# A window-attention and squared-ReLU kernel: a second batch through seven half-size products, the sinks' values in 64-row matmuls, and a written-out order

## The chip, the cores and the metric
One core of one Trainium2 chip runs the whole kernel in one launch. The metric is device time in microseconds (us), the median of three executions. The profiler recorded one execution more. TensorE (PE, with its weight loads PEld) multiplies; VectorE (DVE), ScalarE (ACT) and GpSimd (POOL) work on tiles; SyncE (SP) only issues transfers, and POOL and ACT can issue some as well. SBUF is the on-chip memory, PSUM the 8 accumulator banks of 2 KB a partition that matmuls write to.

## The reference
Four batches, eight heads, 768 positions, 64 channels a head. A query sees the 128 newest keys up to its own and the first four keys ("sinks"). The result, as 3072 rows of 512, goes through two dense layers with a squared ReLU between.
```python
scores = q @ k.T / 8                     # (4, 8, 768, 768)
keep = (key < 4) | ((0 <= query - key) & (query - key < 128))
a = softmax(where(keep, scores, -1e9))
x = (a @ v).transpose(0, 2, 1, 3).reshape(3072, 512)
h = x @ w_in                             # 512 x 2048
out = maximum(h, 0) ** 2 @ w_out         # 2048 x 512, float32
```
Inputs and output are float32 in DRAM.

## The kernel before
**Units.** A batch is 6 query tiles of 128, taken as 3 pairs of tiles; its 8 heads are 4 pairs of heads m = 0 to 3, the two heads of a pair lying in partitions 0-63 and 64-127. Matmuls take bf16.

**Loads.** Batch 0's first four tiles of q and k come by eight SP loads ("qr", L557). Everything else comes by loads that POOL issues and that turn float32 into bf16: tiles of q and k (L578, and L606 for batches 2 and 3), of v (L587, L616), w_in in four parts of 512 KB (L514), w_out in four quarters of 512 KB (L522). POOL's order is: v tiles 0 and 1, w_in part 0, v 2 and 3, w_in parts 1 to 3, k and q tiles 4 and 5, v 4 and 5, w_out 0 to 3, then batch 1 (k, q, v), 2 and 3.

**Attention.** q and k are transposed: batches 0 and 1 on TensorE against `ident` (L708; regrouped first for the SP-loaded ones, copied from PSUM afterwards, L397 to L403), batches 2 and 3 by SP's transposing DMAs (L662). Scores of a pair of heads (L815) are matmuls over 64 rows, one head in each half of the array; ScalarE takes exp (L836); VectorE (L845) or POOL (L426) masks it. Batch 0's first pair of tiles gets its mask as a bias instead, by matmuls with `ident` (L808). The scores of the four sink keys of all heads stand in 32 rows for each pair of heads (L774), their exp in `es` (L782); `vs` holds the sinks' v, zero outside the rows that belong to a head (L756).

**Values** (L884), one PSUM bank a pair of heads: for each head and each of two query tiles up to three matmuls of 65 columns (64 channels and the row sum), the last of them over the sinks, with all 128 rows of `es` and `vs`:
```python
if t >= 2:
    mms.append((i, h2, es[:, 128 * (t - 2):128 * (t - 2) + 128], vs[:, h, :]))
```
VectorE divides (L900, L901). The result is transposed into `xT` by TensorE (L933, a "bridge", batches 0 and 1) or by SP's DMAs (L915, batches 2 and 3).

**First dense layer.** Batches 0 to 2: plain matmuls (L965), 256 columns for batch 0, 512 for the first two pairs of the others and 256 for the third; relu L976 (ACT) or L978 (DVE), square L985 (ACT) or L987 (DVE). Batch 3, named by `FAST = (3,)`: Strassen's seven half-size products. Five sums of quarters of w_in are made once (L1009), four sums of x for each part (L1043, the first a "spread" copy for the single pair); then `quad` makes groups of seven products (L1085): product 1 is copied away (L1126), products 2 and 5 are subtracted from the copy, 4 and 3 are accumulated on 2 and 5, relu (L1141) and square (L1107 on ACT, L1109 on DVE) give two of four blocks, and products 6 and 7 with an add-and-clamp (L1153) and a second square give the other two. A batch has six groups: two of 128 columns for one pair of tiles, four of 256 for two pairs.

**Second dense layer.** The first two pairs of tiles of batch 0 plainly (L1174, store L1197), all others by seven products in Winograd's form: sums of w_out L1215, sums of the squares L1242, products L1284, PSUM combinations L1309 to L1332, stores L1352 to L1371.

**Order.** Every step is registered in a class `Plan` with its engine, modelled cost, dependences and buffers; `Plan.run` then places the steps one after the other by a list scheduler with modelled times, after a table `SHIFTS` has moved the due times of single steps. That gives each engine's program order. `warm` (L386 to L395) puts unneeded matmuls ("dummies", L393) into modelled gaps of TensorE near the start, 63 in all. PSUM is two pools of two tiles of two banks, `den` (dense layers) and `att` (attention). In SBUF `expm` has 8 buffers, `r` 3, `sg` 4; a pool gives its buffers in turn.

Of the kernel before, what the change touches and what calls it, by code (L numbers as in the profile page):

```python
# [12 lines left out]
FP32 = mybir.dt.float32  # L13
BF16 = mybir.dt.bfloat16
# [3 lines left out]
LATENCY = 0.135  # L18
PE_SLACK = 0.0
DMA_START = {"sp": 1.45, "act": 1.2, "pool": 1.6}  # L20
DMA_LATENCY = 0.9
WARM_UNTIL = 34.0
SHIFTS = {
    None: ((-0.254, -0.2), (-0.571, -0.26), (-3.153, 0.8), (-0.345, -0.74), (-0.83, 3.28), (-0.98, -0.76),
        (1.458, 1.69), (-1.232, 0), (0.55, -0.13), (-1.841, -0.16), (-0.527, -1.31), (-1.271, -0.72), (-0.963, 0.32),
        (0.605, -2.77), (-1.323, 1.3), (-1.6, 0.58), (-2.678, -2.44), (-1.476, -0.28), (-2.561, -0.7),
        (-1.331, -0.42), (-1.151, -0.2), (-1.253, -0.22), (-0.398, -0.87), (0.902, 2.55), (-1.318, -0.7),
        (-1.389, -0.4), (-1.246, -0.74), (-0.947, 8.2), (-1.272, 0.2), (-0.428, -2.57), (-1.738, 0), (-1.257, -0.22),
        (-0.151, -1.78), (0.73, -2.69), (-1.258, -0.08), (-1.109, 1), (-1.269, -0.18), (-0.332, -1.95),
        (-1.198, 0.88), (-1.403, -0.28), (-0.085, 0.43), (-1.257, -0.22), (-1.492, -0.14), (-1.966, -0.82),  # L30
        (-1.228, 2.28), (-0.609, -0.3), (-1.172, -0.72), (-0.948, 1.33), (-1.214, -0.14), (-0.818, 0.07),
        (0.509, 0.34), (-1.258, 0.66), (-1.614, 0.1), (-0.282, -0.76), (-0.521, -1.37),),
    ('prep', 0, 0): ((-0.212, 1.23), (-0.072, -0.24), (-0.19, 0.16), (-0.726, 0.34), (0.102, 1.1), (-0.535, 0.02),
        (-0.602, -0.59), (0.354, 0.3), (-3.718, -4.59), (0.634, 0.85), (-0.293, -1.06), (-1.346, -1.52),
        (-0.272, 0.1), (0.418, -0.32), (-0.151, 0.16), (-0.447, -0.7), (0.314, -0.72), (0.319, 0.77), (-0.551, 0.09),
        (-0.072, 0.2), (-0.13, 0.16), (0.105, 0.24), (1.083, 0.83), (0.872, 0.89), (-0.583, 0.42), (-0.732, -0.4),),
    ('sink', 0, 0): ((4.752, 1.43), (1.667, 2.03),),
    ('att', 0, 0): ((0.347, 0.31), (0.954, 0.9), (-0.499, -1.83), (0.762, -2.15), (0.932, -0.05), (-2.305, -7.94),
        (-0.09, 0.64), (-0.608, -0.19),),
    ('val', 0, 0): ((-0.669, 0.31), (-0.697, -0.27), (2.439, -2.91), (-0.554, 0.35), (-0.437, -0.15), (-0.471, 0.35),  # L40
        (-0.386, 0.35), (-0.377, 0.25),),
    ('turn', 0, 0): ((1.726, 0.79), (1.562, 0.69), (1.948, 1.13), (1.496, 0.73),),
    ('att', 0, 1): ((3.244, 0.46), (11.783, 1.08), (3.403, 0.48), (2.622, -0.1), (0.081, -0.49), (-0.044, -0.15),
        (11.287, 1.58), (1.317, -0.32), (2.357, -0.58), (1.537, 1.18), (-0.135, 0.19), (-0.111, -0.81),),
    ('val', 0, 1): ((-1.139, 2.3), (-0.295, 1.56), (-0.887, 1.68), (-0.625, 1.18), (-3.257, -5.22), (-3.374, -3.06),
        (-3.291, -3.92), (-2.551, -2.62),),
    ('turn', 0, 1): ((0.396, -1.51), (-0.815, -0.63), (-0.017, -0.23), (-0.694, 0.15), (-0.252, 1.39),),
    ('prep', 0, 1): ((0.244, -0.3), (0.839, 0.68), (-0.246, 0.32), (0.932, -0.62), (1.027, -0.56), (0.209, -0.32),),
    ('sink', 0, 1): ((1.975, -1.87), (0.782, -1.52),),
    ('att', 0, 2): ((0.244, -0.66), (-1.989, 0.29), (-0.493, 0.33), (0.159, -0.68), (1.032, 0.54), (0.796, 0.57),  # L50
        (-0.189, 0.02), (1.388, -0.12), (0.48, -0.01), (0.313, -0.14), (1.032, 0.72), (-1.933, -0.09),),
    ('val', 0, 2): ((-0.074, -1.39), (-0.782, 0.91), (-0.843, -3.97), (-0.333, 0.47),),
    ('turn', 0, 2): ((0.672, -0.31), (-0.118, -0.09), (0.809, -0.71), (2.596, 0.84),),
    ('l1', 0, 0): ((1.946, 1.98), (2.477, 2.05), (2.842, 0.55), (1.744, 2.15), (1.004, -3.64), (-0.401, 3.09),
        (1.762, -0.33), (2.032, -0.69), (0.818, -0.26), (0.463, 0.08), (2.529, 0.93), (3.08, -0.59),),
    ('l1', 0, 1): ((-1.505, -0.48), (0.385, 0.7), (-1.5, -0.46), (0.416, -0.68), (-0.498, 0.3), (-0.582, 0.6),
        (-0.46, -0.02), (-0.566, -0.1), (0.513, -0.12), (-0.444, -0.02), (-1.914, 1.12), (-0.022, 0.42),),
    ('l1', 0, 2): ((1.159, -0.13), (1.171, -0.31), (4.523, 0.49), (0.77, -0.87), (1.53, -0.41), (0.926, -0.79),
        (0.522, -0.76), (1.124, -0.01), (1.066, -0.47), (4.319, 0.45), (0.749, -2.99), (0.301, -1.88),),
    ('prep', 1, 0): ((-3.284, 0.24), (-1.096, -0.94), (0.605, -0.58), (0.247, -2.12), (-5.483, 0.49), (0.694, 0.02),  # L60
        (0.597, -0.24), (0.597, -0.24), (-8.208, 1.17), (0.681, -1.4), (-1.5, -0.64), (0.357, -0.54), (-10.29, 0.97),
        (0.494, -0.72), (0.633, -0.24), (-0.776, -0.16), (0.529, -0.04), (-1.768, -0.84),),
    ('sink', 1, 0): ((0.868, 0.19), (0.763, 0.03),),
    ('att', 1, 0): ((-0.287, -0.2), (-4.964, -0.65), (-1.435, -0.81), (-3.607, -0.91), (-2.001, -0.01),
        (-0.447, -0.1), (-0.674, 0.1), (-0.719, -0.6), (-0.604, 0.18), (-0.781, -0.2),),
    ('val', 1, 0): ((-6.954, 1.31), (0.072, -4.26), (-0.107, -0.44), (-0.058, -0.46),),
    ('turn', 1, 0): ((-4.522, 0.82), (-0.734, 2.5), (-1.073, 0.44), (0.276, 0.05),),
    ('att', 1, 1): ((1.003, 0.22), (1.223, 0.6), (0.413, -0.45), (0.232, -0.07), (0.259, -0.21), (0.322, -0.07),
        (1.914, -1.56), (0.055, 0.01), (0.085, -2.03), (0.176, 0.47),),
    ('val', 1, 1): ((0.205, 0.29), (-0.249, -0.53), (-2.761, 0.71), (0.377, -0.27),),  # L70
    ('turn', 1, 1): ((0.754, 1.22), (2.068, -0.78), (0.857, 1.68), (-4.788, 1.81),),
    ('prep', 1, 1): ((2.397, 1.96), (5.859, 1.94), (-0.449, 1.75), (1.83, 1.58), (1.97, 1.7), (0.173, -0.21),),
    ('sink', 1, 1): ((0.987, -0.02), (-0.036, -5.62),),
    ('att', 1, 2): ((1.119, -4.28), (0.959, -0.36), (0.499, 1.02), (0.438, -0.34), (1.738, -0.38), (0.767, 0.25),
        (1.547, -0.3), (1.332, 0.31), (1.014, 0.54), (0.269, -2.08),),
    ('val', 1, 2): ((1.128, -0.41), (3.047, 0.37), (3.469, 0.88), (2.416, -3.47),),
    ('turn', 1, 2): ((-4.356, -7.65), (-0.607, -0.19), (-1.006, 0.46), (-4.587, -4.53),),
    ('wt', 0): ((-0.423, 0.42), (-0.315, 0.14), (-1.716, 1), (-0.361, 0.06),),
    ('l2', 0, 0): ((6.071, 1.48), (1.943, -1.23), (2.592, 0.39), (0.401, -1.21), (5.784, 0.74), (5.992, 1.58),
        (2.993, -2.81), (2.732, 0.86), (0.489, -0.39), (-0.516, -1.21), (2.415, 0.45),),  # L80
    ('l2', 0, 1): ((-0.438, 1.25), (-0.215, 0.46), (-0.282, 0.35), (0.307, -0.75), (-0.329, 0.71), (0.749, -0.74),
        (0.871, 0.46), (0.785, 0.08), (0.702, 1.69), (-0.352, 0.8), (2.254, -2.28),),
    ('sum', 0, 2): ((0.045, -1.68), (0.204, -1.02), (-0.718, -2.55), (0.064, -1.38),),
    ('l2', 0, 2): ((0.177, 0.43), (0.08, 0.05), (0.043, -0.01), (0.087, 0.13), (0.146, -0.05), (0.286, 0.01),
        (-3.566, 0.64),),
    ('ev', 0, 2): ((0.387, -2.73), (0.215, -1.01), (-0.063, -1.45), (-0.129, -4.69), (0.419, -1.95), (0.228, -0.91),
        (-0.334, -3.43), (0.529, -0.75),),
    ('l1', 1, 0): ((-2.25, 1.33), (0.301, 1.9), (2.02, -1.38), (0.412, 0.1), (0.164, 0.26), (0.039, -0.22),
        (0.926, -8.17), (-0.524, 0.12), (0.373, 0.12), (1.304, 1.55), (1.015, 0), (0.579, -0.12), (0.204, -0.09),
        (0.523, 0.4), (-0.028, -0.17), (-1.901, 0.85), (0.353, 0.12), (0.196, 0.02), (-1.978, -2.11), (1.417, -0.02),  # L90
        (0.319, -0.99), (0.194, -4.07), (-3.291, 0.39), (0.291, 2.35),),
    ('l1', 1, 2): ((2.497, -0.43), (3.349, 0.01), (2.786, -0.17), (2.851, -0.17), (2.812, 1.03), (0.807, 1.08),
# [106 lines left out]
        (0.268, 1.28),),  # L199
    ('ev', 3, 2): ((1.463, 6.42), (-1.377, 1.64), (0.142, -5.03), (-0.286, -3.32), (-0.494, 0.4), (-0.624, -0.94),  # L200
        (-0.804, -0.94), (-1.227, -0.94), (-0.047, -3.46),),
}


class Slot:
# [16 lines left out]
class Plan:  # L222

# [1252 lines left out]
```

## Time and profile before

| | us |
|---|---|
| median of three executions | 217.82 (217.82, 218.05, 216.72) |
| profiled execution: span from the first to the last instruction | 216.0 |
| busy: PE / PEld / DVE | 206.5 / 165.4 / 161.5 |
| busy: ACT / POOL | 123.2 / 98.7 |
| landed: the last of the eight q and k loads of SP | 11.3 |
| landed: v 0, v 1, w_in part 0 | 11.8, 12.8, 16.2 |

The profiled execution's own time is its span; the median of the executions is 1.8 above it. How to read the lines shown below: in a wait's line stand the waiting engine, tile and line, what it waited for, and then the us in all, the number of times, and the longest. In the chain of work that ended last a line has a start, a length and what ran. A window's line has its two ends, its length, the busy time of PE, PEld, DVE, ACT and POOL with their instructions, the granted TensorE clock, the share that the transfers kept the DMA engines busy (over 1 when several stand queued), and GB/s. A timeline's line has start, length, engine, kernel line, operation, tile and operands. A group's line has line, engine, operation, operands, count, then busy us and mean ns of one, then the idle time before them and who ended it. A matmul's record is longer than its share of the pipeline: what one costs in a row is the distance of the starts.

### The profile page before, as it was taken

The page shows a single profiled execution, that of the slowest core. Times are in us where ns is not written, and L with a number is a line of the kernel's source. Part 1 is how long each engine was busy: PE and PEld are TensorE (multiplying, and loading weights), DVE is VectorE, ACT ScalarE, POOL GpSimd, SP SyncE. Part 2 cuts the span into 40 slices and gives each one's busy share as a digit, 9 for nine tenths or more (in the row PEclk, how much of TensorE's full clock was granted, in tenths as well). Part 3 has the DMA queues.
Part 4 walks back from the last instruction along what each step waited for, and adds up shares of the span by engine and source line. Part 5 has one row for each costly group of instructions (what it writes and reads, how often), then busy time and mean ns, then how long its engine had stood idle before and what let it go on. Part 6 is the DMA issues. An engine that isn't in the chain of part 4 may idle for free.

```text
span 216.0 us, 5470 instructions
## 1 busy us (share of the span) xinstructions
PE 206.5 (96%) x2287; PEld 165.4 (77%) x2287; DVE 161.5 (75%) x292; ACT 123.2 (57%) x158; POOL 98.7 (46%) x137
## 2 busy tenths in 40 slices
PE   3999999999999999999999999999999998999993
PEld 3858996689486755688887965598898998897882
DVE  6487458773958569688689994477995859999973
ACT  2498567366663775976757268566623369482100
POOL 7799773698935974898954424002302000000000
PEclk9999999999999999999999999999999999999999
DMA  5999999999997699999999936000023260000133
GB/s 156 261 182 206 174 199 213 160 154 205 156 147 169 88 147 133 167 108 147 142 199 133 139 84 209 3 0 0 3 97 75 52 219 3 2 0 5 55 132 107
DMA packets 93625, 26.09 MB, mean 121 GB/s; under 512 B 86816, under 2 KB 91552, under 8 KB 93600
## 3 DMA queue, kind: packets, MB, share of 16 engines
q0 software_dynamic: 69248, 12.59, 80.3%
q1 hardware_dynamic: 24168, 13.07, 28.1%
q8 instruction: 18, 0.29, 0.6%
q10 hardware_dynamic: 184, 0.07, 0.1%
q14 instruction: 7, 0.06, 0.1%
HBM read 27.30 MB, written 6.29 MB: 156 GB/s over the span
## 4 chain that ended last, share of the span: by engine, by line
PE 73%; DVE 14%; ACT 3%; DMA 3%; issue 3%; SPq 2%; DVEq 0%; ACTq 0%
PE pm L965 29%; PE py L1284 20%; PE po L884 6%; PE py L1174 6%; PE ps L815 5%; PE pm L1085 4%; DMA qr<-in_q_dram 3%; DVE sg L1242 3%; ACT expm L836 2%; DVE t L1126 2%; DVE r L1153 2%; SPq L557 2%; PE px L933 1%; DVE gT_sb L1109 1%; DVE expm L848 1%
## 5 line engine op out<-in xcount | busy, mean ns | idle before, releaser
L965 PE MATMUL pm<-xT,w_in_sb 128*128 128x256 bf16 (+1 forms) x448 | 66.1, 304 | 0.0
L965 PEld LDWEIGHTS <-w_in_sb 128*128 128x128 bf16 x448 | 48.3, 114 | 13.4 <-issue 1.3
L836 ACT ACTIVATE expm<-ps 128x1024 bf16<-128x1024 f32 (+1 forms) x48 | 43.7, 951 | 18.1 <-PE ps L815 17.5
L426 POOL TENSOR_SCALAR_AFFINE_SELECT expm<-expm 128x512 bf16<-128x512 bf16 x36 | 27.3, 787 | 55.9 <-ACT expm L836 43.7
L976 ACT ACTIVATE r<-pm 128x1024 bf16<-128x1024 f32 x30 | 30.7, 1023 | 17.3 <-PE pm L965 15.6
L1284 PEld LDWEIGHTS <-gT_sb 128*128 128x128 bf16 x336 | 31.2, 98 | 4.3 <-issue 0.7
L987 DVE TENSOR_TENSOR gT_sb<-r 128x1024 bf16<-128x1024 bf16 x26 | 19.3, 741 | 17.3 <-ACT r L976 17.1
L1284 PEld LDWEIGHTS <-sg 128*128 128x128 bf16 x240 | 22.4, 98 | 4.5 <-DVE sg L1242 1.0
L1284 PE MATMUL py<-wt,sg 128*128 128x256 bf16 x160 | 20.8, 273 | 0.4 <-DVE sg L1242 0.4
L1284 PE MATMUL py<-wt,gT_sb 128*128 128x256 bf16 x160 | 20.8, 273 | 0.0
L1284 PE MATMUL py<-w_out_sb,gT_sb 128*128 128x256 bf16 x144 | 18.5, 273 | 0.0
L884 PEld LDWEIGHTS <-expm 128*128 128x128 bf16 x352 | 16.3, 97 | 2.5 <-issue 0.7
L901 DVE TENSOR_TENSOR xn_sb<-po,rc 128x512 bf16<-128x512 f32 (+1 forms) x28 | 17.2, 615 | 1.0
L884 PE MATMUL po<-v,expm 128*128 128x65 bf16 x352 | 17.5, 193 | 0.3 <-DVE xT L402 0.2
L1174 PE MATMUL py<-w_out_sb,gT_sb 128*128 128x512 bf16 x64 | 15.3, 380 | 0.0
L848 DVE TENSOR_TENSOR expm<-expm,tri 128x1024 bf16<-128x1024 bf16 x14 | 11.0, 791 | 5.1 <-ACT expm L836 4.9
L815 PE MATMUL ps<-qkT 64*128 64x256 bf16 (+1 forms) x256 | 14.6, 238 | 0.0
L815 PEld LDWEIGHTS <-qkT 64*128 64x128 bf16 x256 | 8.1, 94 | 7.1 <-issue 6.1
L884 PE MATMUL po<-vs,es 128*128 128x65 bf16 x128 | 12.9, 193 | 0.0
L400 ACT ACTIVATE osb<-py 128x256 f32<-128x256 f32 (+1 forms) x15 | 6.6, 441 | 10.2 <-PE py L1284 7.1
L884 PEld LDWEIGHTS <-es 128*128 128x128 bf16 x128 | 11.7, 97 | 0.0
L587 POOL DMA_DIRECT2D v<-in_v_dram x12 | 11.0, 927 | 0.2
(97 smaller groups left out, 330.5 us busy)
## 6 DMA issues: line engine op xcount, KB each, us to landing
out_dram<-osb SPq DMA_DIRECT2D x11, 512.0 KB, 3.7
v<-in_v_dram POOLq DMA_DIRECT2D x24, 128.0 KB, 7.5
qn<-in_k_dram POOLq DMA_DIRECT2D x20, 128.0 KB, 7.5
qn<-in_q_dram POOLq DMA_DIRECT2D x20, 128.0 KB, 7.4
w_in_sb<-in_moe_w_in_dram POOLq DMA_DIRECT2D x4, 512.0 KB, 10.3
w_out_sb<-in_moe_w_out_dram POOLq DMA_DIRECT2D x4, 512.0 KB, 10.2
qr<-in_k_dram SPq DMA_DIRECT2D x4, 256.0 KB, 5.7
qr<-in_q_dram SPq DMA_DIRECT2D x4, 256.0 KB, 5.3
```

The lines of the kernel that those rows point to most:

```text
L426: nc.gpsimd.affine_select(out=e_tile, in_=e_tile, compare_op=ALU.is_ge, fill=fill, base=i - 1, pattern=[[0, n], [1 if i else -1, 128]], ch ...
L587: return [nc.gpsimd.dma_start(out=v_sb[b % 2][:, t, :, 0:D], in_=v[b, :, 128 * t:128 * t + 128, :].rearrange("h p d -> p h d"))]
L815: nc.tensor.matmul(ps[:, h2, o:o + w], lhsT=qkT_sb[r, m, 1, c, :], rhs=qkT_sb[r, m, 0, qb:qb + w // 128, :], start=(i == 0 and not biased) ...
L836: nc.scalar.activation(out=x[:, :, o:512], in_=bank_t["s", b, s, m][:, :, o:512], func=AF.Exp, scale=scale)
L848: nc.vector.tensor_mul(y, y, tri.rearrange("p (o a) c -> p o (a c)", o=1).to_broadcast([128, 4, 256]))
L884: touch(("po", b, s, m0), e, nc.tensor.matmul(pv[:, i, h2, :], lhsT=lhsT, rhs=rhs, start=(n_ == 0), stop=(n_ == len(mms) - 1)), j)
L901: touch(("po", b, s, m0), e, nc.vector.tensor_tensor(out=xn_sb[:, 2 * s:2 * s + 2, 128 * (m0 + j0):128 * (m0 + j0 + nj)].rearrange("p i (j ...
L965: nc.tensor.matmul(pm[:, i, :], lhsT=w_in_sb[:, fb // 4, kb, fb % 4:512:4], rhs=xT[:, c0 // 256:(c0 + cw) // 256, kb, :], start=(kb == 0), ...
L976: nc.scalar.activation(out=o, in_=h, func=AF.Relu)
L987: nc.vector.tensor_mul(g, r, r)
L1174: touch((b, u), e, nc.tensor.matmul(pm[:, i, :], lhsT=gT_sb[:, fb, 128 * t:128 * t + 128], rhs=w_out_sb[:, fb, :], start=(fb == 0), stop=( ...
L1284: ins = nc.tensor.matmul(y_, lhsT=x[:, i, :], rhs=r_, start=(first or tail and n == 2) and i == 0, stop=i == HB - 1, skip_group_check=not ...
```

## The change
1. `FAST = (2, 3)`: batch 2's first dense layer is done by six groups of seven products, as batch 3's. The sums of w_in are made before it; sums 6 and 7 now overwrite two quarters of `w_in_sb`, the other three lie where q and k of batch 0 were.
2. The sinks' part of the values becomes a step of its own ahead of the window's part, for the second and third pair of tiles: four matmuls of 130 columns (two heads at once) over 64 rows, the two pairs of heads in the two halves of the array. To that end the pairs m and m+2 share a PSUM tile where m and m+1 did, and the dense layer takes x's four blocks in the order 0, 2, 1, 3.
3. The scheduler, its costs and `SHIFTS` are gone. A string `ORDER` names the steps one by one with their engine (`109p` is step 109 on PE, `+7` puts seven dummies ahead of it, 39 in all), and it fixes the order on each queue. POOL's loads now begin: w_out quarter 1, (constants,) w_out quarter 3, q tiles 4 and 5, v tile 4, v 0 and 1, k tiles 4 and 5, w_in part 0, v 3, 2 and 5, w_in part 2, k tile 0 of batch 2 and q tile 0 of batch 1, w_in part 3, k tile 0 of batch 1, w_in part 1. SP's eight loads bring heads' pairs 0, 2, 1, 3. On TensorE the first values stand behind the transposes of all four pairs of heads.
4. Every buffer is a pool of one; a step takes the buffer that came free first in program order. PSUM is one pool of four two-bank tiles for everything; `expm`, `r` and `sg` become one pool of 15 buffers (`w2`). Which step takes which buffer is thereby fixed by `ORDER` too.
5. Some relus, squares and copies go to another of the engines that can do them.

```diff
-    sizes = dict(att=2, den=2, qr=5, qs=6, expm=8, r=3, osb=2, sg=4, u=2)
+    sizes = dict(ps=4, qr=5, qs=6, w2=15, osb=2, u=2)
...
+    def run(self, order):
+        free = {p: list(range(n)) for p, n in self.capacity.items()}
+        emitted = set()
+        for word in order.split():
+            n, _, dummies = word.partition("+")
+            o, e = self.ops[int(n[:-1])], {"p": "pe", "v": "dve", "a": "act", "g": "pool", "s": "sp"}[n[-1]]
+            for s in o.takes:
+                s.buf = free[s.pool].pop(0)
+            self.dummies = int(dummies or 0)
+            o.run(e)
+            for s in o.reads:
+                s.readers -= 1
+                if not s.readers:
+                    free[s.pool].append(s.buf)
...
-                                        if t >= 2:
-                                            mms.append((i, h2, es[:, 128 * (t - 2):128 * (t - 2) + 128], vs[:, h, :]))
...
+                        def sinks(e, s=s, m0=m0, bo=bo):
+                            po = bank_t["o", b, s, m0] = tile_of(bo, "po", [128, 2, 512], FP32)
+                            for i in range(2):
+                                for j in range(2):
+                                    r, m, c = slice(64 * j, 64 * j + 64), m0 + 2 * j, 128 * (2 * s + i - 2)
+                                    touch(("po", b, s, m0), e, nc.tensor.matmul(
+                                        po[:, j, 2 * (D + 1) * i:2 * (D + 1) * (i + 1)].rearrange("p (h d) -> p h d", h=2),
+                                        lhsT=es[r, c:c + 128], rhs=vs[r, 2 * m:2 * m + 2, :],
+                                        start=(i == 0), stop=False), j)
...
-                for kb in range(NKB):
+                for kb in (0, 2, 1, 3):
...
+                if n >= 3:
+                    wi_sb[name] = [x[:, 0], x[:, 1]]
+                    nc.vector.tensor_tensor(out=x, in0=x, in1=y, op=how)
...
-    NATURAL, TURNED, BIASED, FAST = (2, 3), (), 1, (3,)
+    NATURAL, TURNED, BIASED, FAST = (2, 3), (), 1, (2, 3)
...
-    P.place(SHIFTS)
-    P.run()
+    P.run(ORDER)
```

## The prediction
> **What bounds the kernel now.** I read the page first (engines, chain), then TensorE's waits, then matmuls in order of time, then the busy time by stretches, and at the end the groups by shape for prices.
>
> ```profile
> span 216.0 us, 5470 instructions
> PE 206.5 (96%) x2287; PEld 165.4 (77%) x2287; DVE 161.5 (75%) x292; ACT 123.2 (57%) x158; POOL 98.7 (46%) x137
> PE 73%; DVE 14%; ACT 3%; DMA 3%; issue 3%; SPq 2%; DVEq 0%; ACTq 0%
> ```
>
> TensorE is the bound, and 73% of the chain that ended last is its own work. What it waits for is little once it has started:
>
> ```profile
> PE pt L393 <- POOL ident L450: 3.5, 1, 3.5
> PE pm L1085 <- DVE xs L1043: 0.5, 1, 0.5
> PE py L1284 <- DVE sg L1242: 0.4, 1, 0.4
> PE pm L1085 <- DVE t L1126: 0.4, 2, 0.2
> ```
>
> After the first line, which is the start, no entry is over 0.5 us. So a gain has to come from less matmul work, and a loss can come from any place that makes TensorE wait. Two places matter. The first is the head, where the chain starts with a load:
>
> ```profile
> 4.50 6.82 DMA qr<-in_q_dram
> ...
> 17.36 1.87 PE pm L965 x16
> 20.83 1.75 PE pm L965 x16
> ```
>
> The last of the eight q and k loads lands at 11.3; the dense layer begins at 17.4 and from there TensorE is full. The second is the dense layer of batch 3, the one place where half-size products run now: the window 178:200 below has VectorE at 20.83 of 22 us and TensorE at 20.60. The GB/s column of the other rows gives the loads' rates: q and k alone (3:8), w_out alone (30:38), tiles of 128 KB alone (52:56).
>
> ```profile
> 3.00:8.00 5.00, 4.48 (x43) 4.49 (x44) 2.95 (x7) 1.03 (x2) 4.84 (x9) 1.00 0.88 264
> 8.00:11.00 3.00, 3.00 (x47) 2.27 (x46) 1.51 (x3) 2.19 (x4) 2.01 (x6) 1.00 1.53 239
> 30.00:38.00 8.00, 8.00 (x87) 5.76 (x85) 5.98 (x10) 6.36 (x9) 4.07 (x6) 1.00 1.06 214
> 52.00:56.00 4.00, 3.94 (x48) 2.56 (x46) 2.46 (x7) 2.55 (x5) 3.22 (x4) 1.00 2.43 156
> ```
>
> ```profile
> 178.00:200.00 22.00, 20.60 (x190) 18.79 (x188) 20.83 (x30) 14.09 (x18) 0.00 (x0) 1.00 0.01 2
> ```
>
> **Part 1: batch 2's first dense layer.** Removed: 64 matmuls of 512 columns and 64 of 256. The chain has 8 of 512 in 1.73 us and 16 of 256 in 1.75, so 8 x 1.73 + 4 x 1.75 = 20.8 us. Added: six groups of seven products, two groups of 128 columns (8 matmuls a product at 56 ns, 0.45 us) and four of 256 (4 at 109 ns, 0.44 us): 14 x 0.45 + 28 x 0.44 = 18.6 us. TensorE gains 2.2 us, all of it on the path.
> Beside it VectorE gets 12 subtractions of 0.68 (8.2), 6 sums with the clamp of 1.22 (7.3) and the sums of inputs (3.2), and gives 14 squares and sums of 0.74 to others: with a few moved copies about +12 us, to 173. ScalarE gets 14 more squares of 1.05, 6 copies of 0.60 and one of 1.05, less 7 relus of 1.02 and some copies: about +10, to 133. The cover is thin in one stretch. In the new order, from the middle of batch 1's second layer to the last group of batch 3, TensorE has 80 us of work; VectorE's instructions there, count by mean, times 161.5/172.2 (the page's busy time over count by mean) make 81 us. In 178:200 VectorE was at 95% and TensorE lost 1.4 of 22 us. I take 1.5 us of new waits for this stretch; the ends are 0 and 7 (80 us at the 6% of that window, 5, and 2 more for dependences).
>
> **Part 2: the sinks.** Removed: 128 matmuls of 65 columns; 24 of their kind take 0.73 us in the chain, 30 ns each, 3.9 us. Added: 16 groups of four matmuls of 130 columns over 64 rows. That two such run at once is seen in the scores, which have 64 rows too:
>
> ```profile
> 60.35 1.04 PE L1284 MATMUL py<-w_out_sb,gT_sb 128*128 128x256 bf16 x8
> 61.32 0.61 PE L815 MATMUL ps<-qkT 64*128 64x128 bf16 x12
> 61.87 1.05 PE L1284 MATMUL py<-wt,sg 128*128 128x256 bf16 x8
> ```
>
> The 12 hold 2048 columns, 0.85 us one after the other at 0.417 ns; the next group begins 0.55 us after them, so pairs run together (0.43) and 0.12 is lost at the way out; on the way in 0.10 is lost (60.35 + 8 x 0.109 = 61.22, and the scores start at 61.32). A sink group is then 2 x 54 ns, 0.11 us, and 16 are 1.7 us: 2.2 less. But the program's order now goes into 64 rows six times more and out eight times more: 6 x 0.10 + 8 x 0.12 = 1.6 us. Net -0.6. The Trainium skill speaks against this part (TensorEngine Tiling (Array Packing), Tiling Modes): changing the tiling mode drains the array. The two gaps above agree with it; without the drain the part would be worth 2.2 us. If the pairs did not run together it would cost 1.1 us instead.
>
> **Part 3: the order, in the head.** GpSimd's queue now starts with two quarters of w_out, then q tiles 4 and 5, v tile 4, and only then v tiles 0 and 1, which the first values need; before, v 0 and 1 came first (landed at about 12). TensorE's order has the transposes of the last q and k (loads 7 and 8) before the first values, and the scores of the last pair behind them. So the first values wait for all q and k and for all loads up to v 1. In 8:11 both queues were moving, at 239 GB/s, no more than one alone: the transfers share. Traffic begins at 2.0 us (2.10 MB in 264 GB/s is 7.9 us), w_out 2 x 0.52 MB at 214 is 4.9, five tiles of 0.131 MB at 156 are 4.2: 19.0. If mixing gains a tenth, 17.4. I take 18.3. The Trainium skill (DMA: Bandwidth & Descriptors, Issuing engines are not separate DMA queues) says the same of queues of different engines: they run on the same 16 DMA engines and interleave; with separate ones the values would start near 14.
> What is queued behind: on TensorE, after two groups of values (0.36), biased scores (0.7), then ScalarE in order has two exps of 0.81, three of 1.02, two of the sinks (0.38), a copy (0.60) and an exp of 1.02 before the first dense matmul gets its PSUM buffer, which is now fixed to the one that this exp frees:
>
> ```profile
> L836 ACT ACTIVATE expm<-ps 128x1024 bf16<-128x1024 f32 x32 | 31.5, 1021 | 13.2 <-PE ps L815 12.6
> L836 ACT ACTIVATE expm<-ps 128x768 bf16<-128x768 f32 x16 | 12.4, 809 | 4.9 <-PE ps L815 4.9
> L976 ACT ACTIVATE r<-pm 128x1024 bf16<-128x1024 f32 x30 | 30.7, 1023 | 17.3 <-PE pm L965 15.6 <-DVE gT_sb L987 1.4
> ```
>
> Together 0.36 + 0.7 + 7.0 = 8.1. w_in part 0 (four tiles' and its own time behind v 1, 4.3 us) and v 2 and 3 (6.1) are earlier than that, the next w_in parts too. The first dense matmul starts at 18.3 + 8.1 = 26.4. Until then TensorE will have streamed 8.3 us of columns (counted in the new program, dummies left out). The kernel before had streamed as much at 20.2. So the head costs 6.2 us; ends 3.5 and 9.5 (the two ends of the loads, and 0.7 either way in ScalarE's chain).
>
> **Part 4: what costs nothing.** FIFO buffers and one PSUM pool only change who waits for whom, which is in Part 3. SyncE's transposes of batch 2 and 3 and GpSimd's later loads move ahead; loads end earlier than the 121 us of now, since the order of the tiles changes and not their number (tiles land 0.9 us apart). Of TensorE's small waits between 20 and 172 us (about 1.5 us in all) I take most as gone, since every other engine has 6 us more lead there: -1.5, between -1.5 and +1.5.
>
> **Sum**, against the profiled execution: 216.0 - 2.2 - 0.6 + 6.2 + 1.5 - 1.5 = 219.4, of which I keep 219.2 (some of the drains fall in the head's idle time). The median of the three runs, 217.82, is 1.8 above this span, so 221.0 us, slower by 1.5%.
>
> **Rivals.**
> A, the head is not held (faster). If the loads are through when TensorE gets to the values, ScalarE alone sets the start of the dense layer: 15.3 us of its instructions from the first landed q, about 5.0, is 20.3, no loss. For it: the dense layer's own loads are early in both kernels. Against it: 17.4 us is the least that the measured rates give. Time 216.0 - 2.8 + 0.1 = 213.3, with 1.8 around it 215.1. It decides from a first dense matmul before 21.
> B, VectorE becomes the bound in the 80 us stretch, beside the late head: 5.5 us more, 226.5. For it: 81 us against 80, an in-order engine. Against it: 95% was sustained over 22 us at a loss of 1.4.
> C, the clock. The first 42 dummies of the profile run at 107 ns, half speed, up to 8.1 us, although the windows print 1.00; the new order has 39 dummies in all and long idle times in the head. If the clock stays at half until 4.5 us into the dense layer (dummies began at 3.5), that costs 2.3 more: 223.3. The Trainium skill (TensorE: Matmul & The Clock Gate, Part 1) has the clock halved by default and again after an idle window of about 3.4 us; the dummies agree with the first, and no run here shows the second.
>
> **How the numbers follow.** Forecast 0.40 (its own range 218.5 to 223.5), A 0.38, B 0.12, C 0.10. The three repeats of now differ by 0.6%, so about 1% can be told from no change. Faster by over 1% (below 215.6): four fifths of A, 0.30. Slower by over 1% (above 220.0): most of the forecast, B and C, 0.48. Within: 0.22. The range leaves a tenth on either side: at the bottom A without its new waits (213.6) and with the first dense matmul 1.1 earlier, 212.5; at the top B, 226.0.
>
> **What would show it.** Right: the first dense matmul after 25 us, the first values waiting on a v or qr load, v 0 and 1 landing after 17; gaps of 0.10 and 0.12 around sink groups; six groups of products in batch 2 of 3.1 us; VectorE at 90% or more from 120 us on. Wrong: qr and v both landed by 14, a dense layer from 20 or 21 us on, or TensorE's waits in the second half adding up to over 6 us.

## The result, and the profile after

The changed kernel took 225.11 us (median of four executions, 222.21 to 227.03) beside 217.94 for the kernel before: slower. The ratio is 1.025, with an interval of 1.021 to 1.029. Set again beside the last experiments, it took 225.58 (223.39 to 228.65, six executions) beside 217.71: ratio 1.034, 1.030 to 1.038. The ratios leave out the slowest executions (two of the four and two of the six), so they lie under the quotients of the medians; the first profile below (227.03) is of one that is left out, the second (223.39) is not. The change costs 2.5 to 3.4%; the forecast was 221.0, 1.5%.

The page of the first profiled execution, span 225.3 (busy time, and the chain's shares):

```profile
PE 204.1 (91%) x2291; PEld 167.7 (74%) x2295; DVE 167.4 (74%) x310; ACT 129.6 (58%) x168; POOL 98.6 (44%) x136
...
PE 62%; DMA 17%; DVE 10%; POOL 5%; issue 1%; SPq 1%; ACT 1%; DVEq 0%; ACTq 0%
```

TensorE is busy 2.4 us less, so the change did save matmul time; but transfers, 3% of the chain before, are now 17% (10% in the second profile). TensorE's waits:

```profile
PE pt L426 <- DVE qs L182: 6.1, 1, 6.1
PE pt L426 <- POOL ident L225: 4.9, 1, 4.9
PE ps L530 <- DMA qkT<-qn: 3.0, 1, 3.0
PE ps L530 <- ACT osb L180: 1.2, 1, 1.2
PE py L1025 <- DVE sg L983: 0.9, 1, 0.9
```

The first two are the head (the kernel before waits for `ident` too, 3.5 us, but not over 0.5 for a regrouped tile). The third is new and lies at 79 us. VectorE's sums, which the prediction feared in the second half, stand at 0.9. The head in the timeline (start, length, what, and in brackets the idle time before it):

```profile
15.01 0.61 PE L426 MATMUL pt<-ident,qs 128*128 128x128 bf16 x4 [6.06 <-DVE qs L182]
...
21.63 0.53 PE L609 MATMUL po<-v,expm 128*128 128x65 bf16 x12
...
29.13 1.91 PE L686 MATMUL pm<-xT,w_in_sb 128*128 128x256 bf16 x16
```

L426 are the transposes of q and k, L609 the first values, L686 the first dense matmuls. TensorE stood still for 6 us for a regrouped k tile; in the chain that tile's load takes 11.64 us:

```profile
2.86 11.64 DMA qr<-in_k_dram
```

The eight loads of q and k end at 17.8 (11.3 before), v 1 lands at 21.58, and 0.05 us later the first values run. In this profile TensorE, at half clock until about 21 us, had only just come to them. In the second profile it comes to them at 20.51 and has to wait for v 1:

```profile
21.42 0.46 PE L609 MATMUL po<-v,expm 128*128 128x65 bf16 x10 [0.67 <-DMA v<-in_v_dram]
```

To compare the two kernels along the way I summed the columns that TensorE's records stream (0.417 ns each as the unit of account, which is what 8 of 512 in 1.73 us come to within 2%; side by side ones half; dummies left out) and read off when each reaches the same sum (four records of 512 columns that the changed kernel's traces lack are put in). Three later runs stand beside them:

| useful work, us | before | changed | changed, again | run 9 | run 10 | run 11 |
|---|---|---|---|---|---|---|
| 8.3 | 19.9 | 28.2 | 28.0 | 28.6 | 20.3 | 22.1 |
| 30 | 42.7 | 51.3 | 50.7 | 51.4 | 44.1 | 44.8 |
| 35 | 47.9 | 56.4 | 55.9 | 56.5 | 53.7 | 50.0 |
| 55 | 69.4 | 78.1 | 77.6 | 78.2 | 75.6 | 71.7 |
| 60 | 75.0 | 88.5 | 84.8 | 84.2 | 81.4 | 87.7 |
| end (span) | 216.0 | 225.3 | 221.7 | 222.2 | 223.6 | 225.4 |

So the 9.3 us are: +8.3 in the head (28.2 - 19.9), +0.4 from there to 55 us of work (49.9 against 49.5), +4.8 between 55 and 60 (10.4 against 5.6), -4.2 from there to the end (136.8 against 141.0). The last is about what the fewer columns give: 4.3 us, counted in the programs. In the second profile of the same kernel the four are +8.1, +0.1, +1.6 and -4.1, together 5.7; a ratio of 1.025 is 5.4 us.

The step at 55 to 60 us of work is the wait on batch 2's transposed q and k. First the changed kernel's first profile, then its second:

```profile
78.99 0.34 PE L530 MATMUL ps<-qkT 64*128 64x128 bf16 x4
82.28 0.72 PE L530 MATMUL ps<-qkT 64*128 64x128 bf16 x8 [2.95 <-DMA qkT<-qn]
82.93 1.89 PE L1025 MATMUL py<-wt,sg 128*128 128x256 bf16 x8
```

```profile
78.42 0.34 PE L530 MATMUL ps<-qkT 64*128 64x128 bf16 x4
80.24 0.45 PE L530 MATMUL ps<-qkT 64*128 64x128 bf16 x8 [1.48 <-DMA qkT<-qn]
80.63 1.05 PE L1025 MATMUL py<-wt,sg 128*128 128x256 bf16 x8
```

The same eight products take 1.89 us after a wait of 2.95 and 1.05 after one of 1.48: the longer wait dropped the clock to half (the granted clock of the window 78 to 86 is 0.79). So between these two executions a wait that is 1.5 us longer costs 3. That it makes the spread of the others too is not shown: the fastest of the first four (222.21) had a mean granted clock of 0.975, the slowest (227.03) one of 0.992. What the scores waited for, in the first profile's chain:

```profile
66.06 7.29 DMA qn<-in_k_dram
73.35 8.89 DMA qkT<-qn
...
82.28 0.72 PE ps L530 x8
```

A transposing DMA that is issued at 73.35 lands 8.89 us later, among GpSimd's tile loads. It brings k tile 3: the changed order starts batch 2 with the second pair of tiles, after 55.8 us of work. The kernel before starts it with the first pair, at 73.62 after 59.0 us, without a wait, and comes to the other pairs only from 95.04 on, after 78.7:

```profile
73.62 0.51 PE L815 MATMUL ps<-qkT 64*128 64x256 bf16 x8
...
95.04 0.62 PE L815 MATMUL ps<-qkT 64*128 64x128 bf16 x12
```

The sinks' part, priced in Part 2, as it runs (a dense layer ahead, the window's values behind):

```profile
120.77 0.49 PE L686 MATMUL pm<-xT,w_in_sb 128*128 128x256 bf16 x3
121.19 0.40 PE L584 MATMUL po<-vs,es 64*128 64x130 bf16 x8
121.53 0.66 PE L609 MATMUL po<-v,expm 128*128 128x65 bf16 x16
```

### The profile page after: what moved, and what is told of

Same layout as the page of the kernel before. It is cut to its first block, busy times and chain, and to the rows that moved or that the text cites. A ratio compares the mean times of both kernels' runs of the same rounds, so it can differ in the third digit from the quotient of the medians.

```text
span 225.3 us, 5501 instructions
## 1 busy us (share of the span) xinstructions
PE 204.1 (91%) x2291; PEld 167.7 (74%) x2295; DVE 167.4 (74%) x310; ACT 129.6 (58%) x168; POOL 98.6 (44%) x136
## 4 chain that ended last, share of the span: by engine, by line
PE 62%; DMA 17%; DVE 10%; POOL 5%; issue 1%; SPq 1%; ACT 1%; DVEq 0%; ACTq 0%
PE py L1025 23%; PE pm L686 16%; PE pm L826 14%; DMA qr<-in_k_dram 5%; DMA w_in_sb<-in_moe_w_in_dram 5%; DMA qkT<-qn 4%; DMA qn<-in_k_dram 3%; PE po L609 3%; POOL v L340 2%; PE ps L530 2%; POOL qn L329 2%; DVE r L894 1%; DVE expm L562 1%; PE py L915 1%; POOL expm L199 1%
## 5 line engine op out<-in xcount | busy, mean ns | idle before, releaser
L199 POOL TENSOR_SCALAR_AFFINE_SELECT expm<-expm 128x512 bf16<-128x512 bf16 x36 | 28.3, 822 | 51.4 <-ACT expm L550 51.3
L686 PE MATMUL pm<-xT,w_in_sb 128*128 128x256 bf16 (+1 forms) x320 | 44.0, 294 | 0.1
L686 PEld LDWEIGHTS <-w_in_sb 128*128 128x128 bf16 x320 | 34.4, 114 | 6.2 <-issue 0.7
L697 ACT ACTIVATE r<-pm 128x1024 bf16<-128x1024 f32 x18 | 18.0, 1023 | 18.3 <-PE pm L686 18.3
L826 PE MATMUL pm<-xs,w_in_sb 128*128 128x128 bf16 (+1 forms) x256 | 25.0, 246 | 0.0
L340 POOL DMA_DIRECT2D v<-in_v_dram x24 | 21.4, 905 | 3.4 <-PE po L609 3.3
L1025 PE MATMUL py<-wt,sg 128*128 128x256 bf16 x160 | 21.6, 280 | 1.0 <-DVE sg L983 0.9
L329 POOL DMA_DIRECT2D qn<-in_k_dram x20 | 18.1, 912 | 9.9 <-DVE qs L182 5.7
L826 PEld LDWEIGHTS <-w_in_sb 128*128 128x128 bf16 x256 | 21.9, 114 | 0.6 <-issue 0.3
L530 PE MATMUL ps<-qkT 64*128 64x128 bf16 (+1 forms) x256 | 15.8, 249 | 4.1 <-DMA qkT<-qn 3.0
L329 POOL DMA_DIRECT2D qn<-in_q_dram x20 | 17.9, 899 | 1.9 <-DMA w_out_sb<-in_moe_w_out_dram 1.0
L848 ACT ACTIVATE gT_sb<-r 128x1024 bf16<-128x1024 bf16 x18 | 18.3, 1057 | 0.1
L826 PEld LDWEIGHTS <-qkT 128*128 128x128 bf16 x192 | 16.4, 114 | 0.1
L867 DVE TENSOR_TENSOR t<-t,pm 128x512 f32<-128x512 f32 x24 | 15.4, 679 | 0.3 <-PE pm L826 0.3
```

Source lines behind the costliest of these rows:

```text
L199: nc.gpsimd.affine_select(out=e_tile, in_=e_tile, compare_op=ALU.is_ge, fill=fill, base=i - 1, pattern=[[0, n], [1 if i else -1, 128]], ch ...
L329: nc.gpsimd.dma_start(out=qn_t[b, ti][:, t, :].rearrange("p (h d) -> p h d", d=D), in_=(q, k)[ti][b, :, 128 * t:128 * t + 128, :].rearrang ...
L340: nc.gpsimd.dma_start(out=v_sb[b % 2][:, t, :, 0:D], in_=v[b, :, 128 * t:128 * t + 128, :].rearrange("h p d -> p h d"))
L530: nc.tensor.matmul(ps[:, h2, o:o + w], lhsT=qkT_sb[r, m, 1, c, :], rhs=qkT_sb[r, m, 0, qb:qb + w // 128, :], start=(i == 0 and not biased) ...
L686: nc.tensor.matmul(pm[:, i, :], lhsT=w_in_sb[:, fb // 4, kb, fb % 4:512:4], rhs=xT[:, c0 // 256:(c0 + cw) // 256, kb, :], start=(kb == 0), ...
L697: nc.scalar.activation(out=o, in_=h, func=AF.Relu)
```

## The experiments

In the edits `34g` is step 34 on GpSimd, and so on; line numbers lie up to one lower in these kernels. Theory H: the head is held by the loads ahead of v 0 and 1. Its rival was C: clock and ScalarE hold it.

**Run 1: w_out's quarters 1 and 3 later.**
```diff
-... 13s 34g 56a 5g 4g 3g ... 63p 36g 29g ... 122v 33g 111v ...
+... 13s 56a 5g 4g 3g ... 63p 29g ... 122v 34g 36g 33g 111v ...
```


> The changed kernel with the two quarters of w_out (1 and 3) moved in GpSimd's queue from its start to just ahead of quarter 0. Theory H (the head is held by the loads that stand ahead of v 0 and 1): 1.05 MB at 214 GB/s is 4.9 us, so v 1 lands near 16.7 instead of 21.6, the first dense matmul starts near 24.5 instead of 29.1, and the time falls by 4 to 5 us, to about 220.5. Rival C (TensorE's clock, at half until 21 us, and ScalarE's chain decide the head): v 1 comes earlier all the same, but the first dense matmul moves by less than 1.5 us and the time stays above 223.5.

Measured: 226.08 us. v 1 landed at 16.24 (expected 16.7), the first dense matmul came at 25.02 (expected 24.5), 8.3 us of work at 24.1 instead of 28.2. So H is right on the head and C is not. But the time did not fall. Its waits:

```profile
PE ps L529 <- DMA qkT<-qn: 3.6, 1, 3.6
PE pt L425 <- DMA qn<-in_k_dram: 2.0, 2, 1.4
PE po L608 <- DMA v<-in_v_dram: 1.9, 2, 1.1
```

All are loads: batch 1's k tiles, now behind all of w_out, and the transposes of batch 2, which TensorE reaches earlier. The head's 4 us were given back at later loads.

**Run 2: in addition v 0 and 1, w_in part 0, v 3 and 2 first.**
```diff
-... 29g 30g 31g 68v 19g 20g ... 21g ... 23g 22g ...
+... 19g 20g 21g 23g 22g 29g 30g 31g 68v ...
```


> As the first, and in addition v 0 and 1, w_in part 0, v 3 and 2 stand first in GpSimd's queue, ahead of q tiles 4 and 5 and v 4, as in the kernel before. Theory H: q and k land by 11.5, v 1 by 13, the first dense matmul starts at 20 to 21.5, and the time falls by about 8 us, to 217. Rival C: 221 or more.

Measured: 229.16, slower still. v 1 landed at 12.85, as expected, and then the next load was late:

```profile
20.74 0.29 PE L425 MATMUL pt<-ident,qn 128*128 128x128 bf16 x1 [3.37 <-DMA qn<-in_k_dram]
```

In TensorE's order k tiles 4 and 5 are transposed before the first dense matmul, so that came at 28.85, no sooner than unedited. My expectation had copied the old load order without the old order of use. What makes the run slower still comes later: the wait on batch 2's transposes, with half clock behind it, is longer than in any profile of the unedited kernel.

```profile
PE ps L529 <- DMA qkT<-qn: 4.2, 1, 4.2
```

**Run 3: one transposing DMA of batch 2 earlier in SyncE's queue.**
```diff
-... 385s 388s 17s 387s 390s ... 307s 386s
+... 385s 386s 388s 17s 387s 390s ... 307s
```


> The changed kernel with one transposing DMA of SyncE, that of batch 2's k tile 3, moved ahead of three others and a store that stood before it. Theory S (TensorE's 2.95 us stall at 79.3 is the place of that transfer in SyncE's queue, and the half clock after it is a consequence): it is issued near 68.5, lands by 77, the scores at 79 run without a wait, no matmuls at half rate follow, and the time falls by 4 to 5 us, to about 220.7. Rival (the transfers are saturated there, one late transpose is exchanged for another): a wait of over 1.5 us on the transposed q and k stays between 75 and 90, and the time falls by less than 2 us.

Measured: 227.06. The wait on the transposes went, and right behind those scores another stood, with half clock after it:

```profile
79.12 0.61 PE L529 MATMUL ps<-qkT 64*128 64x128 bf16 x12
82.25 1.86 PE L1024 MATMUL py<-wt,sg 128*128 128x256 bf16 x8 [2.51 <-DVE osb L181]
```

`osb` is the buffer of the stores: step 307, a store of 512 KB, now stood behind one more transpose. So theory S is right that the place in the queue sets the wait, and its price is wrong: an exchange as the rival has it happened, with a store in place of a second transpose.

**Run 4: the edits of runs 2 and 3.** 

> The second and the third edit together. If both theories hold and the parts add: 225.1 - 8 - 4.4 = 212.7, faster than the kernel before by 5 us. If the late transpose was only late because all loads were late (a consequence of the head): the same as the second alone, about 217 less the stall in it.

Measured: 228.68. Both replaced waits are there, and no sum of gains:

```profile
PE pt L425 <- DMA qn<-in_k_dram: 5.7, 3, 4.9
...
PE py L1024 <- DVE osb L181: 3.6, 1, 3.6
```

From here on, theory D: the transfers as a whole pace the first 80 us, because the changed order asks for more of them by a given point of TensorE's work than the DMA engines have brought.

**Runs 5 and 6: cheaper loads, in the changed kernel and in the one before.** Both read other data into each place than the reference does.
```diff
-in_=(q, k)[ti][b, :, 128 * t:128 * t + 128, :].rearrange("h p d -> p h d"))
+in_=(q, k)[ti][b].rearrange("h s d -> (h s d)")[65536 * t:65536 * t + 65536].rearrange(
+    "(p h d) -> p h d", h=H, d=D))
```


> The changed kernel with GpSimd's loads of q and k tiles reading 512 neighbouring numbers for each partition instead of eight pieces of 64: the same bytes, an eighth as many packets, other rows and heads at each place (the output is then not the reference's). Theory D (the first 80 us are bound by the loads: the order asks for batch 2's transposed q and k after 55 us of TensorE's work, and the DMA engines cannot have brought all that stands ahead of them before 82 us): 26 such tiles stand ahead; at the rate of w_out's long rows, 209 to 214 GB/s, a tile takes 0.6 us instead of 0.9, so the point of 56 us of useful work comes 6 to 8 us earlier and the time falls to about 218. Rival (TensorE is held by ScalarE, VectorE and the clock, the loads only look late): less than 2 us.

Measured: 224.18. The wait on batch 2's transposes is gone: 55 to 60 us of work took 6.7 us instead of 10.4 or 7.2. But the head became worse, so the time hardly moved:

```profile
PE pt L426 <- DVE qs L181: 7.6, 1, 7.6
```

SyncE's last q and k load landed at 19.39 (17.81 unedited): GpSimd's q tiles, in longer rows, came in sooner, and SyncE's loads later. The time fell by less than 2 us, as the rival had it. Nor did the loads in between set the pace: 55 us of work came at 78.9 (78.1 and 77.6 unedited), and from 8.3 us of work to there it took 49.5 us, as in the kernel before. For that stretch theory D does not hold.

> The same edit of the loads in the kernel before. Theory D: its order asks for batch 2's q and k only after 69 us of work, at 85 us, so its loads are covered: within 2 us of 217.7. If it falls as much as the changed kernel does, the loads bound both, and they are not what tells the two apart.

Measured: 219.52 beside 217.92, ratio 1.007 (1.005 to 1.010). Within the 2 us: the kernel before gains nothing from cheaper loads. The 85 us of the expectation are scores of batch 1; batch 2's first are at 73.62, after 59.0 us of work, and they do not wait either.

**Run 7: batch 2's first scores later on TensorE.**
```diff
-... 315p 263a 413p 314v ... 416a ... 414a ... 268p 334a 320p ...
+... 315p 263a 314v ... 268p 334a 269v 413p 416a 414a 320p ...
```


> The changed kernel with the first scores of batch 2 (step 413, with their two exps) moved behind about 9 us of other TensorE work that stood after them; no load is moved. Theory D: at that point the transposes have landed, the 2.95 us wait and the 1.6 us of half clock behind it go, and the time falls by 3 to 4.5 us, to about 221. Rival S2 (a fixed order of buffers: each delay comes back at the next step that takes the buffer): a wait of the same length between 80 and 100 us, and the time stays within 1.5 us of 225.

Measured: 225.09, no gain. The wait on the transposes and the half clock are gone, and small waits came instead:

```profile
80.01 1.03 PE L1024 MATMUL py<-wt,sg 128*128 128x256 bf16 x8 [0.96 <-DVE osb L181]
...
83.82 3.61 PE L685 MATMUL pm<-xT,w_in_sb 128*128 128x512 bf16 x16 [0.53 <-ACT xT L179]
```

55 to 60 us of work took 7.2 us. That is 3.2 less than in the first profile of the changed kernel and the same as in the second: where the wait is the small one there is little to win here. The rival was nearer in the time, but its wait of the same length did not come.

**Run 8: Part 1 alone, in the kernel before and its scheduler.**
```diff
-    NATURAL, TURNED, BIASED, FAST = (2, 3), (), 1, (3,)
+    NATURAL, TURNED, BIASED, FAST = (2, 3), (), 1, (2, 3)
...
-            weight_sums_in(b - 0.1, ...)
+            if b == 2:
+                weight_sums_in(b - 0.1, ...)
```
A third line, not shown, finds the first dense step of the batch before by its place in the list and not by its name.


> Part 1 alone: the kernel before, with its scheduler, and batch 2's first dense layer in six groups of seven products. By the prediction's sum TensorE has 2.2 us less; if VectorE's 12 us more are covered there, 215.5; if VectorE is the bound once batch 2's products run beside batch 1's second layer and batch 3's attention (rival B), 219 or more, with VectorE at 95% from 120 us on.

Measured: 256.82. The time is over the 219 of rival B, far over it, but not by that mechanism: VectorE is at 71% of the span and at 82% from 140 to 170 us, not at 95, and TensorE waits for it and for ScalarE again and again:

```profile
PE py L1284 <- DVE sg L1242: 6.1, 3, 3.1
PE pm L1085 <- DVE xs L1043: 5.3, 1, 5.3
PE pm L1085 <- DVE t L1126: 3.6, 6, 2.0
...
PE pm L1085 <- ACT r L1141: 2.8, 4, 1.2
```

The table of shifts in that scheduler belongs to the old set of steps. That this is why the run is so slow was not tested; the run does not measure what Part 1 is worth in a good order.

**Run 9: batch 3's loads behind batch 2's,** beside the unedited changed kernel.
```diff
-... 606g 604g 375g 605g 238g 377g 367g ... 380g
+... 375g 238g 377g 367g ... 380g 606g 604g 605g ... 615g 624s 625s ...
```


> The changed kernel once more, unedited, beside the next two on the same chip. By its four executions 222 to 227. If its time varies because the chain of loads is tight (theory D), the first dense matmul near 29 and a wait on the transposed q and k between 75 and 85 us are there again.

Measured: 225.58; first dense matmul at 28.85, the wait at 80 shown above.

> The changed kernel with batch 3's 17 tile loads, nine of which GpSimd issues between 58 and 80 us, moved behind batch 2's last one, and their transposes after them in SyncE's queue; TensorE's order is untouched. Theory D: with nine tiles of 0.9 us out of the way the transposes of batch 2 land by 77, the scores at 79 do not wait, the half clock behind them goes, and the time falls by 3 to 4.5 us against the unedited one beside it. Rival (the transposes' own cost or SyncE's issue, 1.2 us each, holds them): a wait of more than 2 us stays at that place.

Measured: 224.42, 1.2 us under the unedited one, their intervals (1.027 to 1.035, 1.030 to 1.038) overlapping; the profiled spans (222.2 and 221.7) stand the other way. So no gain can be claimed. The wait on the transposes is down to 0.2 us with TensorE's order untouched, from 1.5 in the unedited kernel beside it. The transposing DMA that it is for, first in the unedited kernel and then in this run:

```profile
71.46 8.73 DMA qkT<-qn
```

```profile
72.63 6.97 DMA qkT<-qn
```

It landed 0.6 us sooner, and TensorE came there 0.7 us later. So by these two profiles batch 3's tiles are a part of what holds it, 1.8 of 8.7 us, and not the whole. Later a new wait took as much as was won:

```profile
126.87 0.67 PE L529 MATMUL ps<-qkT 64*128 64x128 bf16 x12 [1.54 <-ACT expm L549]
```

**Run 10: the edits of runs 1, 7 and 9, and v 4 (`31g`) behind k 5 (`28g`).** 

> All load edits together: w_out quarters 1 and 3 behind (as in the first run), v tile 4 behind k tiles 4 and 5, batch 3's loads behind batch 2's, and batch 2's first scores later in TensorE's order (as in the seventh). Theory D: first dense matmul near 24, no wait over 1.5 us on a load between 30 and 110 us, a span near 216.5 and a time near 218, 7 us under the unedited one and about level with the kernel before. If a wait of VectorE or ScalarE takes their place (as in the runs where one edit was made alone), over 222.

Measured: 225.39. The head is repaired: first dense matmul 21.49, 30 us of work at 44.1 instead of 50.7. Five us of work later 4.4 of these 6.6 us are gone. The chain there:

```profile
37.33 13.20 DMA qn<-in_k_dram
...
50.58 2.46 PE pt L425 x22
```

A k tile of batch 1 that is issued at 37.33 stands behind four quarters of w_out and a tile of batch 2, and lands at 50.54. The next one comes at 120 us, in the chain:

```profile
119.68 2.49 DMA xT<-xn_sb
122.25 1.07 ACT xd L179
123.34 0.29 DVE xs L783
...
123.78 0.70 DVE xn_sb L624
124.53 0.27 PE ps L529
```

SyncE issues the transposes of batch 2's x behind nine of batch 3's, which the edit had put there. VectorE's sums of that x wait, the division behind them in VectorE's order waits with them, and TensorE's scores need the PSUM buffer that it frees: 4.33 us, and half clock.

**Run 11: the loads in the order of use,** with run 7's edit.
```diff
-34g 5g 4g 3g 36g 29g 30g 31g 19g 20g 27g 28g 21g ... 363g 41g 26g 37g ... 370g 43g 33g 35g 365g 38g 45g 39g ...
+5g 4g 3g 29g 30g 19g 20g 27g 28g 31g 21g ... 41g 26g 37g ... 43g 38g 39g 33g 51g 34g 35g 36g 45g ... 53g 363g 365g ...
-383s 382s 392s 16s 384s 381s 385s 388s 17s 387s 390s 307s 386s
+16s 17s 384s 382s 381s 383s 385s 386s 387s 388s 307s 390s 392s
```


> The changed kernel with GpSimd's loads in the order in which TensorE asks for them: q tiles 4 and 5, v 0 and 1, k tiles 4 and 5, v 4, w_in part 0; w_out quarter 0 only behind batch 1's first four k and q tiles, quarters 1 to 3 behind that; ten tiles of batch 2 that stood between batch 1's behind all of batch 1; batch 2's first scores later in TensorE's order (as in the seventh run). Theory D in numbers: what is asked for by 35 us of useful work is q and k of the start (3.4 + 8.0), ten tiles of batch 0 (9.0), w_in (10.2), w_out (9.8) and twelve tiles of batch 1 (10.8), 51.2 us of transfers one after the other; so 35 us of work cannot be reached much before 51, against 56.1 unedited and 54.1 with the loads that were moved as a block. First dense matmul 21.5 to 22.5, 35 us of work at 51 to 53, no wait over 1.5 us at 413's new place, and 3.5 to 5 us less than the unedited kernel's 225.6: about 221. If the gain of the head is gone again by 60 us of work (85.7 there), something else than the loads paces it, and 224 or more follows.

Measured: 226.76, a miss in the time and a hit on the way: first dense matmul 22.95, 35 us of work at 50.0 (expected 51 to 53; part of w_out was not yet asked for), 55 at 71.7 instead of 77.6. Up to there the same steps with the same loads are 5.9 us faster by their order alone, and all of it is won in the head (8.3 us of work at 22.1 instead of 28.0). From there to 35 us of work it took 27.9 us and the kernel before 28.0, so the hit does not show that the sum of the transfers sets the pace. Then:

```profile
71.56 1.03 PE L1024 MATMUL py<-w_out_sb,gT_sb 128*128 128x256 bf16 x8
81.30 1.86 PE L1024 MATMUL py<-wt,sg 128*128 128x256 bf16 x8 [8.70 <-DVE osb L181]
```

```profile
72.29 8.51 DMA out_dram<-osb
```

I had put the store (307) behind eight transposes, and it landed at 80.8. With it ahead of them the 8.7 us and the half clock behind might be saved; that was not run, so whether this order would beat the kernel before stays open.

## Why the prediction was right, and where it was not

**The head: the mechanism was right, its term too small.** The forecast was that the first values wait for all of q and k and for v 1 because two quarters of w_out and five tiles stand ahead or beside. That is what the timelines show (v 1 at 21.58 and values at 21.63; a wait of 0.67 us on v 1 in the second profile), and run 1 confirms it by taking the quarters away. Measured +8.3 and +8.1 where 6.2 stood (and the 20.2 that the prediction read for the kernel before is 19.9 by the count used here). What was mis-sized is the landing of v 1, 21.6 and not 18.3, and there the bytes, not the rate:

```profile
2.00:21.58 19.58, 10.58 (x94) 7.48 (x95) 7.96 (x17) 6.96 (x11) 13.55 (x21) 1.00 1.43 217
```

19.58 us at 217 GB/s are 4.25 MB; the prediction's 3.80 MB in 17.0 us would be 224 GB/s, almost the same. The other 0.45 MB belong to loads that stand behind v 1 in GpSimd's queue (k tiles 4 and 5 and w_in part 0 are issued at 15.6 to 17.4) and moved beside it: 2 us. The prediction counted only what stands ahead, and took 18.3 where its own sum gave 19.0. The term behind it held: 7.5 us from the first values to the first dense matmul, 8.1 said; only it was TensorE's own work in these 7.5 us, not ScalarE's chain.

**Part 4: "what costs nothing" failed.** "SyncE's transposes of batch 2 and 3 and GpSimd's later loads move ahead; loads end earlier" counted when the loads end, not when the new order asks for each. It asks for batch 2's second pair of tiles after 55.8 us of work, the kernel before for its first pair after 59.0 and for the others from 78.7 on. In runs 5 and 9 (cheaper loads, fewer loads ahead) that wait is gone or 0.2 us, but TensorE also came there 1.5 and 0.7 us later than in the second profile. The wait and the clock behind it cost 4.8 us in one profile and 1.6 in the other. This, with 2 us more in the head, is why the kernel lies above the forecast.

**The sum.** Against the 219.2 of the prediction, the first profile's 225.3 is 2.1 more in the head, 4.8 more between 55 and 60 us of work, where the sum has no term, and 0.8 less elsewhere (3.8 us won where the other terms give 3.0). The second profile's 221.7 is 1.9 and 1.6 more and 1.0 less. Both medians lie above the forecast's own range, 218.5 to 223.5. The wide range holds them because rival B, which did not happen, sets its top at 226.0: that part is luck.

**Part 1** is as priced on TensorE (products at 56 and 109 ns, as in the kernel before). The feared stretch cost no more than the 1.5 us taken. VectorE (the third busy time) is full here and TensorE (the first) is too, but for one wait on ScalarE:

```profile
130.00:140.00 10.00, 8.81 (x115) 8.08 (x116) 9.96 (x15) 5.16 (x9) 9.21 (x12) 1.00 0.45 135
140.00:150.00 10.00, 10.00 (x117) 9.54 (x115) 9.97 (x19) 5.84 (x8) 0.00 (x0) 1.00 0.01 2
150.00:160.00 10.00, 10.00 (x105) 9.46 (x104) 9.71 (x15) 8.56 (x12) 0.00 (x0) 1.00 0.00 0
```

So rival B falls. VectorE at 97 to 100% for 30 us lost TensorE almost nothing but that wait.

**Part 2** said -0.6. The records of the 64 sink matmuls show ten runs of them. Six times they bring an entry into 64 rows that the scores did not need anyway, at 98 ns, and six times an exit, at 123. With 27 ns a matmul that is 1.7 + 0.6 + 0.7 = 3.0 us instead of 128 x 30 ns = 3.8: -0.8. The drain of the Trainium skill (TensorEngine Tiling (Array Packing), Tiling Modes) is there in the trace and takes 1.3 of the 2.1 us that the narrower matmuls save.

**Rival A** (the head is not held) falls by the timeline. **Rival C** had the right fact at the wrong place: transposes run at 107 ns until about 21 us in the first profile, but the values wait for v 1 anyway. In the second profile full speed began at about 18, and 8.3 us of work came only 0.2 us sooner. So half clock costs next to nothing there; it costs 1.6 us behind the wait at 79.

**What stays open:** part of the spread between executions. The two profiles of one kernel differ by 3.6 us, 3.2 of them at that wait; what decides which it is was not found. No order that was run gives the 5 to 7 us back. Loads bind the changed kernel at single points (the head, batch 1's k tiles in runs 1 and 10, batch 2's transposes at 79); that the transfers as a whole pace the first 80 us, as theory D has it, is not borne out by runs 5 and 11.

## What to carry to other kernels

Set up, for each point of the busy engine's work, the sum of all transfers that must have landed by then, and hold it against the clock: an order of matmuls is only as good as the worst of these points, and curing one point (runs 1, 3, 7, 10) shows the next. A load, a transposing DMA and a store that lie in one queue, or on the same DMA engines, are one resource; whoever moves one writes down which other then comes later and who waits for that. A gain counted in columns is safe only if the order that brings it does not ask for data sooner.

## What the runs showed of the hardware

- The clock falls back to half after short waits of TensorE. Half rate followed idle times of 2.04 (run 8, at 124.94), 2.51 (run 3), 2.95, 3.37 (run 2), 4.33 (run 10) and 8.70 us (run 11), and TensorE worked 3 to 6 us at it; after 1.48 and 1.54 the next products ran at full rate. After 4.20 (run 2, at 84.14) the first eight scores still ran at full rate and the products behind them did not. In run 10 it also followed two waits of 0.43 and 1.62 with one transpose between them. The Trainium skill (TensorE: Matmul & The Clock Gate, Part 1) puts the idle window at about 3.4 us; here a wait of 2.0 was enough.
- A transposing DMA of one tile landed 8.9 us after its issue at 73.35, while GpSimd's tiles were moving, and 2.4 us after it at 164.9, alone. A store of 512 KB behind eight of them took 8.5 us (run 11), 3.5 in the page's median.
- SyncE's eight loads of q and k ended at 11.3, 17.8 or 19.4 us, by what GpSimd's queue had in flight (the kernel before, the changed one, run 5): SyncE's queue had no right of way here. The Trainium skill (DMA: Bandwidth & Descriptors, Issuing engines are not separate DMA queues) has transfers interleave whichever engine started them, and the three times agree.
